# One copy of h's spectrum in HBM, a set order on GpSimd around the last group, and operand blocks in the place of u and v

## The chip, the cores and the metric

The kernel runs on one core of a Trainium2 chip. The metric is the device time of one execution in microseconds. Before the change it is 2052.42 us, the median of three runs (2049.76 to 2053.55). Every detail below comes from one further execution that was recorded by the hardware profiler.

The core's engines are named as in the profile: PE is TensorE (matrix products; PEld is its loading of weights), DVE is VectorE, ACT is ScalarE, POOL is GpSimd and SP is SyncE, which here only issues transfers. Each engine works through its own list of instructions in order. Transfers are issued by SP (one hardware queue, q1 in the profile) and by POOL (the software queue, q0).

## The reference

Two parts follow each other. The first is a long causal convolution of eight sequences (5696 tokens, 128 channels) with one filter per channel. The second turns each value by an angle that depends on the token, mixes all tokens with two 5696 x 5696 matrices, and ends with a small layer over channels.

```python
L = 2 * S
Xf = np.fft.rfft(x, n=L, axis=1)
Hf = np.fft.rfft(h, n=L, axis=0)
Yf = Xf * Hf[None, :, :]
y = np.fft.irfft(Yf, n=L, axis=1)[:, :S, :]

theta = y @ w_theta
zr, zi = y * np.cos(theta), y * np.sin(theta)
yr = np.einsum('ts,bsd->btd', w_tok_r, zr)
yi = np.einsum('ts,bsd->btd', w_tok_i, zi)
u = y + yr + yi
out = u + np.maximum(u @ w_ch, 0.0)
```

## The kernel before

**The convolution** (0 to about 395 us) is a Fourier transform of 11392 points, written as matrix products: 178 by 64 points, of which 90 frequencies of the long factor are kept. Work goes in eight groups: two batches (`bp`) times half of the channels (`dh`, 64 of 128), in the order of `groups` (L127). Each group goes through four stages. Stage a (L241 to 258) multiplies x by the first transform's matrix (L250). Stage b (L395 to 410) does the second factor (`f2`, L268), copies the result to `xs` (L402) and multiplies it by h's spectrum `hs`, once as it is and once with its halves swapped, into `u_t` and `v_t` (L404). Stage c (L412 to 431) transforms back (L422, L423), stage d (L433 to 460) finishes and writes the result `yt` (L448). While a group is in its stages c and d, the next group's stages a and b are woven between (`woven`, L278; L729 and L738).

`load_x(g)` (L130) fetches a group's x in 16 transfers on POOL, in narrow rows, into a tile of which there is one only. So the loads of a group wait until TensorE has read the last of the group before.

**h's spectrum** is computed once for all 128 channels. The half for the first 64 channels goes to `hs`. The half for the other 64 (`h_later`) goes to HBM, to `hf_hbm`, by `h_store` (L335): each chunk is written twice, as it is and with its two 64-row halves exchanged, since stage b needs both. When group 3 has used `hs` for the last time with the first half of the channels, each chunk is overwritten by one load from `hf_hbm` (L408).

**The phase steps** (L680) take 128 tokens and four batches each: a transpose by TensorE (L693), five groups of products that give the angle with its whole turns removed (L519 to L536), sine and cosine on ACT (L541 to L543), two products on DVE that give `zz` (L554, L555). A copy of the transposed y goes to HBM as `y2` (L698, L699). The 22 steps of the first four batches (`steps0`, `hh` = 0) stand among the last group's stages c and d and right behind; they read `ya0` and store zz to `z_hbm` (L572). The 22 steps of the other four batches (`steps1`, `hh` = 1) read `ya1`, whose last quarter comes straight from the last group's `yt` (`load_ya1`, L660: two transfers at L673 on SP). The rest of `yt` goes to `yt_hbm` on POOL, behind a one-element copy on POOL that is called the gate (L453 to L459) and that waits for ya1.

**Mixing** takes the rest. Weight tiles come from HBM into a ring of six slots (`load_w`, L625: four transfers on POOL for each slot; for the first six slots a one-element copy stands ahead that waits for a `zz`, L630), are transposed by DVE (L831) and multiplied with the operand blocks `b0` to `b10` (L1137, later L1216). A block holds the zr and zi of its tokens. `load_b_half` (L763) loads the half that the steps of `hh` = 0 have left in `z_hbm`; the steps of `hh` = 1 write their half straight into the blocks (L568). The products of the first blocks are interleaved with the steps of `hh` = 1. Block 0 lies in the ring's tile; blocks 1 to 6 come from a pool opened at L744 and get their places in the order in which they are asked for, at the earliest free address. In the profiled execution block 7's place fell into the space of `ya0`.

**What sets the order.** A scheduler orders each engine's instructions, except on the engines and in the stretches that `tc.manual_schedule` names, where the order of the program stays. Around the last group POOL is in the scheduler's hands, so a load can be put ahead of a copy that stands before it in the program. The transfers of each queue use eight semaphores in turn, so that an issue also waits for the transfer eight before it.

Of the kernel before, what the change touches and what calls it, by code (L numbers as in the profile page):

```python
# [23 lines left out]
def kernel(  # L24
# [66 lines left out]
    CN = 10  # L91
    CHN = [(c0, min(CN, N2 - c0)) for c0 in range(0, N2, CN)]
    UVW = 2 * HD * K1
    hf_hbm = nc.dram_tensor("hf_hbm", (P, UVW), F16, kind="Internal").ap()
    yt_hbm = nc.dram_tensor("yt_hbm", (D, B, S), BF16, kind="Internal").ap()

    psp = ExitStack()
# [221 lines left out]
    def halves(t, c, n, lo=0):  # L319
        return t[:, 2 * HD * CHK[c][0] - lo:2 * HD * (CHK[c + n - 1][0] + CHK[c + n - 1][1]) - lo].rearrange(  # L320
            "p (c r n) -> p c r n", c=n, r=2)
# [11 lines left out]
            nc.sync.dma_start(own[p0:p0 + 64, :, 1], own[64 - p0:P - p0, :, 0])  # L333

    def h_store(c, n):  # L335
        to = halves(hf_hbm, c, n)
        own = h_later[:, HD * CHK[c][0]:HD * (CHK[c + n - 1][0] + CHK[c + n - 1][1])].rearrange(
            "p (c n) -> p c n", c=n)
        nc.sync.dma_start(to[:, :, 0], own)
        for p0 in (0, 64):  # L340
            nc.sync.dma_start(to[p0:p0 + 64, :, 1], own[64 - p0:P - p0])

    r_u = fc.tile([P, P], F16)
    r_v = fc.tile([P, P], F16)
# [50 lines left out]
    def stage_b(a_st, warm, refill):  # L395

        def chunk(c):
            c0, ck = CHK[c]
            hv = h_part(c)
            ps = f2(a_st, c, warm)  # L400
            xs = fs.tile([P, 2, HD, CK], F16, tag="xs", name="xs")
            nc.scalar.activation(xs[:, :, :, :ck], ps, AF.Copy)  # L402
            for r in range(2):
                nc.vector.tensor_tensor(  # L404
                    uv[r][:, :, :, c0:c0 + ck], xs[:, :, :, :ck],
                    hv[:, r:r + 1].to_broadcast([P, 2, HD, ck]), op=mult)
            if refill:
                nc.sync.dma_start(h_flat(c),  # L408
                                  hf_hbm[:, 2 * HD * c0:2 * HD * (c0 + ck)])
        return [lambda c=c: chunk(c) for c in range(NCK)]  # L410

    def stage_c(st, last):  # L412
# [20 lines left out]
    def stage_d(st, bp, dh, then=None):  # L433
        def chunk(n0, cn):
            if n0 == 0:
                st["yt"] = fy.tile([P, NB, N2], BF16, tag="yt", name="yt")
            g_, yt = st["g"], st["yt"]
            ps = psum()
            nq = 5 if cn == CN else cn
            for j in range(cn):  # L440
                n = n0 + j
                o = ps[:, j // nq, (j % nq) * NB:(j % nq + 1) * NB]
                for ri in range(2):
                    e_ = e_t[:K1, n, ri, :] if n < EN else e_t[:K1, N2 - n, ri, ::-1]
                    nc.tensor.matmul(o, g_[:K1, ri * N2 + n, :], e_, start=(ri == 0), stop=(ri == 1))
            y_out = yt[:, :, n0:n0 + cn].rearrange("p m (a q) -> p m a q", q=nq)
            y_in = ps[:, :cn // nq, :nq * NB].rearrange("p a (q m) -> p m a q", q=nq)
            nc.scalar.activation(y_out, y_in, AF.Copy)  # L448
            if n0 + cn == N2:
                if then is not None:  # L450
                    then(yt)
                if then is not None:
                    gate = nc.gpsimd.tensor_copy(small(0, 1)[HD:HD + 1], sides["phases"][1][HD:HD + 1, 3, H - 1:H]).ins  # L453
                for e in range(2):
                    t0 = H if then else 0
                    with tc.issue_after(gate) if then else ExitStack():
                        (nc.gpsimd if then else nc.sync).dma_start(
                            yt_hbm[dh * HD:(dh + 1) * HD, 2 * bp + e, t0:],
                            yt[64 * e:64 * e + 64].rearrange("p m n -> p (m n)")[:, t0:])  # L459
        return [lambda n0=n0, cn=cn: chunk(n0, cn) for n0, cn in CHN]  # L460

    zz_n, rm_n = [0], [0]
# [22 lines left out]
    for n, f in enumerate(a0):  # L485
        f()
        if n == 9:
            e_table(*E_STEPS[0])
    e_index(*E_STEPS[4])
    load_x(1)  # L490
    in_order.close()
    in_order.enter_context(tc.manual_schedule(engines={mybir.EngineType.DVE, mybir.EngineType.Activation}))
    woven(b0, ([s_table, lambda: r_table(0, r_u), lambda: r_table(1, r_v)], 0.0, 0.6),
# [121 lines left out]
    def small(at, n):  # L615
        return ring["all"][:, WB + BT + at:WB + BT + at + n]
# [43 lines left out]
    def load_ya1(yt=None):  # L660

        st = sides["phases"]
        if yt is None:
            a_ = fa.tile([P, 2 * K1, HD], F16, tag="a", name="ya1")
            ya = st[1] = a_.rearrange("p k d -> p (k d)")[:, :4 * H].bitcast(BF16).rearrange(
                "p (b t) -> p b t", b=4)
            for p_ in range(2):
                nc.sync.dma_start(ya[:, :2, p_ * 2 * QR:(p_ + 1) * 2 * QR],
                                  yt_hbm[:, 4:6, p_ * 2 * QR:(p_ + 1) * 2 * QR])
            nc.sync.dma_start(ya[:HD, 2:], yt_hbm[:HD, 6:8, :H])  # L670
        else:
            for e in range(2):
                nc.sync.dma_start(st[1][HD:, 2 + e, :],  # L673
                                  yt[64 * e:64 * e + 64].rearrange("p m n -> p (m n)")[:, :H])

    M2, M6, M7, M5, M1, M3, M4 = range(7)
    ORDER = (M3, M4, M5, M2, M1, M7, M6)
    home_of = {}

    def phase_step(ti, hh):  # L680

        st = sides["phases"]
        yT = st[hh][:, :, ti * P:(ti + 1) * P]
# [12 lines left out]

        def copy():
            nc.vector.tensor_copy(y_ap, tpz)  # L698
            (nc.gpsimd if hh else nc.sync).dma_start(y2_hbm[ti].rearrange("p b d -> p (b d)")[:, 512 * hh:512 * hh + 512],  # L699
                          y_ap.rearrange("p b d -> p (b d)"))  # L700

        phases_b(ti, y_ap, 4 * hh, 4, yT, None, None, None, nc.vector, st["turns"], theta_ps=theta_ps,
# [2 lines left out]
    tile_order = []  # L705
    for a in range(6):
        tile_order += [ti for ti in (a, 5 + a, 11 + a, 16 + a) if ti < 22 and ti not in tile_order]
    steps0 = [lambda ti=ti: phase_step(ti, 0) for ti in tile_order]

    def with_load(step, load):  # L710
        def both():
# [3 lines left out]
                pump()  # L715
        return both

    for g, (bp, dh) in enumerate(groups):
        st = {}
        last = g + 1 == len(groups)  # L720
        a_, b_ = front(g + 1, () if g else (5, 11))
        if last:
            for _ in range(3):
# [20 lines left out]
    bpe = [ctx.enter_context(tc.tile_pool(name="bpool_e", bufs=1, side="right", reuse_waits="tile"))]  # L744
    bts_of = {0: [], 1: []}

    def tile_b(p, j, pool):
        t_ = ring["all"][:, WB:WB + BT] if j == 0 else pool.tile([P, BT], BF16, tag=f"b{j}", name=f"b{j}")
        bt = [t_[:, k * 1024:(k + 1) * 1024].rearrange("p (r n) -> p r n", r=2) for k in range(7)]
        bts_of[p].append(bt)  # L750
        return t_
# [527 lines left out]
```

## Time and profile before

| | us |
|---|---|
| median of three runs | 2052.42 |
| profiled execution | 2055.21 |
| its span, first to last instruction | 2053.4 |
| TensorE busy | 1948.2 (95%) |
| VectorE busy | 1574.1 (77%) |
| ScalarE busy | 653.6 (32%) |
| GpSimd busy | 968.2 (47%) |

The mean granted TensorE clock was 0.985 of full speed. A line of a timeline gives the start, the busy time, the engine (a q behind its name: the issue of a transfer), the line of the kernel, the operation, the tile written and the tiles read, the number of instructions taken together, and in brackets the idle time before, with what ended it. By stretches, with TensorE's busy time in each, the clock, and the mean busy share of the core's 16 DMA engines:

| stretch, us | PE busy, us | clock | DMA share |
|---|---|---|---|
| 55 to 60 | 2.20 of 5 | 0.53 | 1.91 |
| 60 to 65 | 0.02 of 5 | 0.50 | 1.73 |
| 65 to 71 | 1.57 of 6 | 0.50 | 0.78 |
| 335 to 350 | 13.56 of 15 | 1.00 | 0.86 |
| 350 to 365 | 12.46 of 15 | 1.00 | 1.19 |
| 395 to 410 | 9.90 of 15 | 0.77 | 0.95 |
| 410 to 425 | 10.31 of 15 | 0.77 | 1.02 |
| 455 to 470 | 12.56 of 15 | 0.94 | 0.94 |

A share above 1 means that transfers overlap in the records of an engine.

### The profile page before, as it was taken

Reading aid. Unit: us, or ns where it says so; the run is one execution under the profiler, and the core shown is the slowest. Engines: PE = TensorE matmul, PEld = TensorE weight load, DVE = VectorE, ACT = ScalarE, POOL = GpSimd, SP = SyncE. Lnnn points to the kernel's source line nnn. Section 1 sums busy time; section 2 is a strip of 40 time slices with the busy share of each in tenths; the row PEclk is TensorE's granted clock in tenths of the full one; section 3 lists DMA queues with packets and bytes.
Section 4 is the critical chain, followed back from the end, with each engine's and each line's share of the span. In section 5 each row is a group of like instructions: output and inputs, shape, how many; then the busy total and the mean of one; then the engine's idle time right before and its main releaser. Section 6 shows DMA issues by size and latency. Waiting matters only on the chain.

```text
span 2053.4 us, 41419 instructions
## 1 busy us (share of the span) xinstructions
PE 1948.2 (95%) x15841; PEld 1072.1 (52%) x15841; DVE 1574.1 (77%) x2890; ACT 653.6 (32%) x1004; POOL 968.2 (47%) x1738
## 2 busy tenths in 40 slices
PE   5699999789999999999999998999999999999998
PEld 5588888544444444444444443444444444444444
DVE  8677778767788888888867667867777686777767
ACT  6688888852333333333300000011111111111111
POOL 9422422274454545454566454453544535354450
PEclk9899999999999999999999999999999999999999
DMA  9968966999999998989999799697887969788793
GB/s 111 95 74 132 88 81 174 221 257 195 170 171 181 169 181 153 181 170 179 170 172 159 117 250 220 105 153 131 149 147 128 157 125 153 131 151 145 128 160 84
DMA packets 492486, 314.03 MB, mean 153 GB/s; under 512 B 182599, under 2 KB 456391, under 8 KB 491303
## 3 DMA queue, kind: packets, MB, share of 16 engines
q0 software_dynamic: 322208, 156.75, 60.5%
q1 hardware_dynamic: 164096, 143.10, 24.4%
q10 hardware_dynamic: 5984, 11.54, 1.6%
q8 instruction: 124, 2.03, 0.4%
q14 instruction: 74, 0.61, 0.1%
HBM read 354.89 MB, written 92.29 MB: 218 GB/s over the span
## 4 chain that ended last, share of the span: by engine, by line
PE 67%; DVE 3%; POOL 1%; issue 1%; DMA 1%; ACT 0%; DVEq 0%; POOLq 0%
PE m L1216 61%; PE m L1137 2%; POOL ring L632 1%; DVE c L1223 1%; DVE b L772 1%; PE utp L911 1%; PE v L918 1%; PE m L1220 1%; DVE wt L831 1%; PE theta_ps L519 0%; PE tpz L859 0%; PE m L1103 0%; DMA wl<-in_moe_w_tok_i_dram 0%; DMA y_hbm<-ring 0%; POOL wl L878 0%
## 5 line engine op out<-in xcount | busy, mean ns | idle before, releaser
L632 POOL DMA_DIRECT2D ring<-in_moe_w_tok_i_dram x720 | 388.1, 547 | 658.2 <-DVE wt L831 576.5
L632 POOL DMA_DIRECT2D ring<-in_moe_w_tok_r_dram x720 | 386.6, 548 | 147.6 <-DVE wt L831 81.6
L831 DVE STREAM_TRANSPOSE wt<-ring 128x384 f32<-128x384 f32 (+2 forms) x720 | 359.9, 525 | 111.9 <-PE m L1216 71.2
L1216 PE MATMUL m<-b,wt 128*128 128x512 bf16 x1640 | 390.5, 380 | 2.0 <-DVE wt L831 1.7
L1216 PEld LDWEIGHTS <-wt 128*128 128x128 bf16 x1804 | 176.5, 98 | 220.1 <-DVE wt L831 7.8
L1223 DVE TENSOR_TENSOR c<-c,m 128x512 f32<-128x512 f32 x412 | 266.0, 671 | 0.4 <-PE m L1216 0.4
L913 ACT ACTIVATE ring<-utp 128x512 bf16<-128x512 bf16 x85 | 50.7, 597 | 582.2 <-PE utp L911 582.2
L137 POOL DMA_DIRECT2D x<-in_x_dram x128 | 99.3, 801 | 140.6 <-PE ps L250 133.3
L422 PE MATMUL ps<-r_u,u_t 128*128 128x128 f16 x1024 | 125.1, 221 | 9.3 <-ACT ph L542 3.4
L423 PE MATMUL ps<-r_v,v_t 128*128 128x128 f16 x1024 | 124.2, 220 | 0.3
L1137 PE MATMUL m<-b,wt 128*128 128x512 bf16 x480 | 113.9, 388 | 10.3 <-DMA b<-z_hbm 5.7
L908 ACT ACTIVATE ub<-c 128x512 bf16<-128x512 f32 x88 | 55.1, 628 | 191.5 <-DMA ring<-in_moe_w_tok_r_dram 112.9
L423 PEld LDWEIGHTS <-v_t 128*128 128x128 f16 x1024 | 100.8, 99 | 7.2 <-issue 6.0
L422 PEld LDWEIGHTS <-u_t 128*128 128x128 f16 x1024 | 100.9, 99 | 5.2 <-DVE u_t L404 4.0
L402 ACT ACTIVATE xs<-ps 128x1024 f16<-128x1024 f32 x96 | 91.8, 988 | 7.2 <-DVE v_t L404 1.6
L1137 PEld LDWEIGHTS <-wt 128*128 128x128 bf16 x528 | 51.6, 100 | 70.2 <-issue 12.2
L404 DVE TENSOR_TENSOR u_t<-xs,hs 128x1024 f16<-128x1024 f16 x96 | 64.0, 666 | 29.7 <-ACT xs L402 26.9
L521 ACT ACTIVATE red<-theta_ps,magic 128x512 f32<-128x512 f32 (+1 forms) x46 | 31.6, 687 | 134.3 <-PE theta_ps L519 97.6
L861 ACT ACTIVATE ring<-tpz 128x512 bf16<-128x512 bf16 (+1 forms) x46 | 27.5, 597 | 130.5 <-PE tpz L859 111.3
L268 PEld LDWEIGHTS <-w_t 64*128 64x128 f16 x3240 | 57.5, 99 | 21.8 <-issue 15.9
L250 PE MATMUL ps<-f_t,x 89*128 89x180 f16 x512 | 53.7, 247 | 11.4 <-DMA x<-in_x_dram 9.4
L404 DVE TENSOR_TENSOR v_t<-xs,hs 128x1024 f16<-128x1024 f16 x96 | 63.4, 661 | 0.0
(2934 smaller groups left out, 3812.1 us busy)
## 6 DMA issues: line engine op xcount, KB each, us to landing
ring<-in_moe_w_tok_r_dram POOLq DMA_DIRECT2D x352, 96.0 KB, 4.6
ring<-in_moe_w_tok_i_dram POOLq DMA_DIRECT2D x352, 96.0 KB, 4.8
ring<-in_moe_w_tok_r_dram POOLq DMA_DIRECT2D x352, 80.0 KB, 4.3
ring<-in_moe_w_tok_i_dram POOLq DMA_DIRECT2D x352, 80.0 KB, 3.7
cp_hbm<-c SPq DMA_DIRECT2D x88, 256.0 KB, 2.4
c<-cp_hbm SPq DMA_DIRECT2D x88, 256.0 KB, 4.5
out_dram<-c SPq DMA_DIRECT2D x88, 256.0 KB, 4.0
yy<-y_hbm SPq DMA_DIRECT2D x84, 128.0 KB, 2.4
```

The costliest lines, as they stand in the source:

```text
L137: nc.gpsimd.dma_start(x16[p0:p1, e, n0:n0 + 16, :HD], bass.AP(tensor=src.tensor, offset=src.offset + (p0 * N2 + n0) * D + dh * HD, ap=[[N2 ...
L268: nc.tensor.matmul(ps[:, e, j * HD:(j + 1) * HD], w_t2[rows, slot(e, c0 + j), N2 * (1 - ri):N2 * (3 - ri)], a_st["a"][rows, ri * K1 + c0 + ...
L402: nc.scalar.activation(xs[:, :, :, :ck], ps, AF.Copy)
L404: nc.vector.tensor_tensor(uv[r][:, :, :, c0:c0 + ck], xs[:, :, :, :ck], hv[:, r:r + 1].to_broadcast([P, 2, HD, ck]), op=mult)
L422: nc.tensor.matmul(o, u_t[:, at:at + P], r_u, start=True, stop=False)
L423: nc.tensor.matmul(o, v_t[:, at:at + P], r_v, start=False, stop=True)
L632: nc.gpsimd.dma_start(wb[32 * i:32 * i + 32, :ng, :nj * 64], bass.AP(tensor=a.tensor, offset=a.offset + row0 * S + p * H + i * QR + j0 * 6 ...
L831: nc.vector.transpose(wt.rearrange("p j t r -> p (j t r)").bitcast(F32).rearrange("p (j g t) -> p g j t", j=TJ, g=4)[:, :ng, :nj], wb[:, : ...
L908: nc.scalar.activation(ub[:m].rearrange("p b d -> p (b d)"), c[:m], AF.Copy)
L1137: nc.tensor.matmul(ms[n // 2 * 2 + h], a[n][:, j, :, r], bts_of[p][jj][n % 2 * 2 + h][:, r, :], start=(n % 2 == 0 and jj == 0 and r == 0), ...
L1216: nc.tensor.matmul(ms[q], a[q][:, j, :, r], bts[jj][q][:, r, :], start=(jj == 0 and r == 0), stop=(jj == NJ - 1 and r == 1 and q not in left))
L1223: nc.vector.tensor_tensor(c, z, ms[q], op=op)
```

## The change

Five things change, all in front of the mixing part:

1. `h_store` writes the second half's spectrum once, in four plain stores; `hf_hbm` is half as large. The reload in group 3 makes the swapped half: three loads for a chunk instead of one.
2. `load_x(1)` stands ahead of the index set `e_index(*E_STEPS[4])` on POOL.
3. From the last group to the end of the steps of `hh` = 0, POOL keeps the order of the program (`late_order`). The gate of L453 is gone.
4. The two `ya` loads from `yt`, and the y2 stores of the steps 12 to 16 of `hh` = 0, are issued by POOL and no longer by SP.
5. The tiles of blocks 1 to 6 are asked for in the order 5, 6, 1, 2, 3, 4, before the loads, which stay in the order 0 to 6. Blocks 1 to 4 thereby get the addresses that `u_t` and `v_t` had.

The order of instructions on DVE and ACT stays. On PE the products on block 1 begin inside the fourth step of `hh` = 1 and no longer behind the sixth; some thirty groups later the two orders agree again. POOL issues the loads of block 1 directly behind the y2 store of the first step of `hh` = 1.

```diff
-    hf_hbm = nc.dram_tensor("hf_hbm", (P, UVW), F16, kind="Internal").ap()
+    hf_hbm = nc.dram_tensor("hf_hbm", (P, HD * K1), F16, kind="Internal").ap()
...
     def h_store(c, n):
-        to = halves(hf_hbm, c, n)
-        own = h_later[:, HD * CHK[c][0]:HD * (CHK[c + n - 1][0] + CHK[c + n - 1][1])].rearrange(
-            "p (c n) -> p c n", c=n)
-        nc.sync.dma_start(to[:, :, 0], own)
-        for p0 in (0, 64):
-            nc.sync.dma_start(to[p0:p0 + 64, :, 1], own[64 - p0:P - p0])
+        part = slice(HD * CHK[c][0], HD * (CHK[c + n - 1][0] + CHK[c + n - 1][1]))
+        nc.sync.dma_start(hf_hbm[:, part], h_later[:, part])
...
             if refill:
-                nc.sync.dma_start(h_flat(c),
-                                  hf_hbm[:, 2 * HD * c0:2 * HD * (c0 + ck)])
+                src = hf_hbm[:, HD * c0:HD * (c0 + ck)]
+                nc.sync.dma_start(h_flat(c)[:, :HD * ck], src)
+                for p0 in (0, 64):
+                    nc.sync.dma_start(h_flat(c)[p0:p0 + 64, HD * ck:], src[64 - p0:P - p0])
...
                     then(yt)
-                if then is not None:
-                    gate = nc.gpsimd.tensor_copy(small(0, 1)[HD:HD + 1], sides["phases"][1][HD:HD + 1, 3, H - 1:H]).ins
                 for e in range(2):
                     t0 = H if then else 0
-                    with tc.issue_after(gate) if then else ExitStack():
-                        (nc.gpsimd if then else nc.sync).dma_start(
+                    (nc.gpsimd if then else nc.sync).dma_start(
...
+    load_x(1)
     e_index(*E_STEPS[4])
-    load_x(1)
...
             for e in range(2):
-                nc.sync.dma_start(st[1][HD:, 2 + e, :],
+                nc.gpsimd.dma_start(st[1][HD:, 2 + e, :],
...
-    def phase_step(ti, hh):
+    def phase_step(ti, hh, store=nc.sync):
...
-            (nc.gpsimd if hh else nc.sync).dma_start(y2_hbm[ti].rearrange("p b d -> p (b d)")[:, 512 * hh:512 * hh + 512],
+            store.dma_start(y2_hbm[ti].rearrange("p b d -> p (b d)")[:, 512 * hh:512 * hh + 512],
...
-    steps0 = [lambda ti=ti: phase_step(ti, 0) for ti in tile_order]
+    steps0 = [lambda ti=ti, n=n: phase_step(ti, 0, nc.gpsimd if 12 <= n < 17 else nc.sync)
+              for n, ti in enumerate(tile_order)]
...
+    late_order = ExitStack()
     for g, (bp, dh) in enumerate(groups):
         st = {}
         last = g + 1 == len(groups)
+        if last:
+            late_order.enter_context(tc.manual_schedule(engines={mybir.EngineType.Pool}))
...
+    place_of = {}
+
+    def new_b(j, pool):
+        return ring["all"][:, WB:WB + BT] if j == 0 else pool.tile([P, BT], BF16, tag=f"b{j}", name=f"b{j}")
+
     def tile_b(p, j, pool):
-        t_ = ring["all"][:, WB:WB + BT] if j == 0 else pool.tile([P, BT], BF16, tag=f"b{j}", name=f"b{j}")
+        t_ = place_of.pop(j) if j in place_of else new_b(j, pool)
...
+    for j in (5, 6, 1, 2, 3, 4):
+        place_of[j] = new_b(j, home_pool(j))
     for j in range(7):
         load_b_half(j)
     for step in steps0:
         step()
+    late_order.close()
...
-    steps1 = [lambda ti=ti: phase_step(ti, 1) for ti in
+    steps1 = [lambda ti=ti: phase_step(ti, 1, nc.gpsimd) for ti in
```

More of the change, by code (lines that the diff above doesn't have):

```diff
@@ L451, in chunk @@
                     then(yt)
-                if then is not None:
-                    gate = nc.gpsimd.tensor_copy(small(0, 1)[HD:HD + 1], sides["phases"][1][HD:HD + 1, 3, H - 1:H]).ins
                 for e in range(2):
                     t0 = H if then else 0
-                    with tc.issue_after(gate) if then else ExitStack():
-                        (nc.gpsimd if then else nc.sync).dma_start(
-                            yt_hbm[dh * HD:(dh + 1) * HD, 2 * bp + e, t0:],
-                            yt[64 * e:64 * e + 64].rearrange("p m n -> p (m n)")[:, t0:])
+                    (nc.gpsimd if then else nc.sync).dma_start(
+                        yt_hbm[dh * HD:(dh + 1) * HD, 2 * bp + e, t0:],
+                        yt[64 * e:64 * e + 64].rearrange("p m n -> p (m n)")[:, t0:])
         return [lambda n0=n0, cn=cn: chunk(n0, cn) for n0, cn in CHN]
@@ L672, in load_ya1 @@
             for e in range(2):
-                nc.sync.dma_start(st[1][HD:, 2 + e, :],
-                                  yt[64 * e:64 * e + 64].rearrange("p m n -> p (m n)")[:, :H])
+                nc.gpsimd.dma_start(st[1][HD:, 2 + e, :],
+                                    yt[64 * e:64 * e + 64].rearrange("p m n -> p (m n)")[:, :H])
     M2, M6, M7, M5, M1, M3, M4 = range(7)
```

## The prediction

> **What bounds the kernel now.** I read the page's totals and its chain first:
>
> ```profile
> span 2053.4 us, 41419 instructions
> PE 1948.2 (95%) x15841; PEld 1072.1 (52%) x15841; DVE 1574.1 (77%) x2890; ACT 653.6 (32%) x1004; POOL 968.2 (47%) x1738
> ...
> PE 67%; DVE 3%; POOL 1%; issue 1%; DMA 1%; ACT 0%; DVEq 0%; POOLq 0%
> PE m L1216 61%; PE m L1137 2%; POOL ring L632 1%; DVE c L1223 1%; DVE b L772 1%; PE utp L911 1%; PE v L918 1%; PE m L1220 1%; DVE wt L831 1%; PE theta_ps L519 0%; PE tpz L859 0%; PE m L1103 0%; DMA wl<-in_moe_w_tok_i_dram 0%; DMA y_hbm<-ring 0%; POOL wl L878 0%
> ```
>
> TensorE is busy for 95%, and the mixing products of L1216 are 61% of the chain. The change does not touch that part; what it can win is TensorE's idle time before it, and a microsecond won there shifts the rest. So I took timelines of two places where TensorE waits, first the wait for the second group's x:
>
> ```profile
> 43.25 0.47 PE L250 MATMUL ps<-f_t,x 89*128 89x180 f16 x4 [0.20 <-ACT a__745 L257]
> ...
> 43.30 0.57 POOL L155 IOTA e_all<- 90x445 f32 x1
> 43.98 0.64 POOL L375 TENSOR_SCALAR e_all<-e_all,lane 90x445 f32<-90x445 f32 x1
> 44.70 1.33 POOL L159 TENSOR_SCALAR e_all<-e_all 90x445 f32<-90x445 f32 x1
> 45.98 6.21 POOL L137 DMA_DIRECT2D x<-in_x_dram  x8
> ...
> 62.80 0.61 POOL L137 DMA_DIRECT2D x<-in_x_dram  x1 [0.23 <-DMA x<-in_x_dram]
> ...
> 65.12 0.38 DVE L404 TENSOR_TENSOR v_t<-xs,hs 128x256 f16<-128x256 f16 x1
> ...
> 69.43 2.00 PE L250 MATMUL ps<-f_t,x 89*128 89x180 f16 x12 [9.41 <-DMA x<-in_x_dram]
> 71.22 0.31 PE L422 MATMUL ps<-r_u,u_t 128*128 128x128 f16 x1
> ```
>
> The index set (three GpSimd operations) stands ahead of the 16 x loads, TensorE waits 9.41 us for the last of these, and stage c (L422), whose operands were complete at 65.5, starts at 71.22. The queues from 44 to 70 us, where h's stores (q1) run beside x (q0):
>
> ```profile
> q0 software_dynamic: 12544, 1.46, 90.4%
> q1 hardware_dynamic: 3584, 3.11, 45.7%
> ```
>
> Then the transition to mixing:
>
> ```profile
> 394.91 0.70 SPq L673 DMA_DIRECT2D ya<-yt  x1
> ...
> 399.23 0.29 PE L693 MATMUL tpz<-ident_bf,ya 128*128 128x128 bf16 x1 [2.92 <-DMA ya<-yt]
> ...
> 401.32 0.39 DVE L698 COPY ring<-tpz 128x512 bf16<-128x512 bf16 x1
> ...
> 407.78 4.32 POOL L767 DMA_DIRECT2D b<-z_hbm  x8 [2.60 <-PE theta_ps L536]
> ...
> 414.69 1.86 PE L1137 MATMUL m<-b,wt 128*128 128x512 bf16 x4 [5.46 <-DMA b<-z_hbm]
> ...
> 422.33 1.03 PE L1137 MATMUL m<-b,wt 128*128 128x512 bf16 x4
> ```
>
> TensorE waits 2.92 us for ya and 5.46 us for the first operand block; the loads of the blocks start only at 407.78, when ya0's last reader (L536) has freed the place of block 7, which stands first.
>
> **The change part by part.** *Set order and h's bytes.* The index set's 2.7 us (43.30 to 46.0) move behind the x loads. These can't start before TensorE's last read of the single x buffer (43.25 + 0.47 = 43.7), so they start 2.2 us earlier. h's 12 stores of 2.95 MB become 4 of 1.47 MB. x(2), loaded with nothing beside it, needs 16 us from first issue (86.97) to the last landing; x(1) needs 23.4. I put the 7.4 us between down to h, and halve them with its bytes: 3.7. x(1) would land at 43.7 + 16 + 3.7 = 63.4, 6.0 us earlier. Next in line is the last v_t at 65.5; with 0.1 us to start, stage c moves from 71.2 to 65.6, its four batches of x products first filling TensorE's wait: **-5.6 us**. Bounds: -2.2 (order alone, h's bytes unfelt) and -5.7. The moved set ends some 2.7 us after x's last issue, at 63.9 even if x's 17.4 us of issuing stay; its reader on VectorE starts at 65.4: 0, and up to +1 if that cover fails. SP's queue only gets shorter here.
>
> *Refill.* 12 loads become 36, in group 3, at 172.9 to about 194. At 0.55 to 0.6 us an issue they are 21 us of SP, behind which two stores of yt wait (before, the last ends at 194.3). Landing takes these up to 7.9 us, and ACT overwrites yt at 212.6; the refilled hs is read at 210.8. Cover of some 10 us: **0**; +3 if the swapped halves go at half speed.
>
> *Ring order of the last group.* Ten of the 24 first ring loads were issued at 338.9 to 344.7, ahead of the copies that gate the rest. Now all follow their gates, from 350.2. The transfers beside them (yt's stores, ya1, y2) then start against an emptier queue, and 350 to 360 gets fuller: from 350 to 365 the DMA share is already 1.19, from 335 to 350 it is 0.86. VectorE waits for y2 stores in these rows, 3.2 us at 361.43 and 1.0 at 364.02. **-1**; bounds -4 (both waits gone) and +2 (as many ring loads as now, later, in the fuller stretch).
>
> *ya and the operand blocks.* yt is complete at 391.5. GpSimd, idle there, can issue the two ya loads at once, ending at 392.7 instead of 395.6 behind z's and y2's stores on SP; with the 3.8 us that ya takes to land, 396.5 instead of 399.2. VectorE gains nothing by that: it is busy without a gap from 392.6 to 401.3, so the first y2 copy of the second half stays at 401.3. Its store, GpSimd's next instruction, issues at 402.3, and b1 behind it at 402.9 instead of 408.4, since block 1 lies where u_t was and waits for no ya0. From issue to landing b1 took 6.3 us (408.4 to 414.7): 409.2. But TensorE's order changes too: the first product on b1 now stands inside the fourth step, three steps earlier. Behind it come the 7.6 us from 414.7 to 422.3 plus three steps of five phase groups at 0.22 us, 3.3 us: 420.1, a gain of 2.2 at a place from which the two orders agree. In those 7.6 us groups took 0.42 us instead of 0.22 (granted clock 0.5); if the shorter wait leaves half of that slowness out, 2.5 us less. I take **-3.5**. Bounds: 0 (b1 lands at 411.4, so 420.1 becomes 422.3) and -8 (landing after 4.9 us, the median of the nearest 128 KB stores on that queue, and no slow stretch).
>
> [...]
>
> *Stores that change queue.* Five y2 stores and two ya loads leave SP, 7 x 0.6 = 4.2 us there, and add 0.55 to 0.6 each to GpSimd, idle 370 to 399 (29.1 us for ya), when most are issued. GpSimd later runs from 427 to 465 almost without pause, about 15 us behind VectorE at 419; loads that begin 5.5 us earlier shrink this. From 455 on TensorE waits 2.54 us for a weight block and 0.94 and 1.15 for the last operand rows, VectorE 1.56 and 1.45 for stores: 4.6 us of TensorE's. **-2**; bounds 0 and -4.
>
> Sum: -5.6 - 1 - 3.5 - 2 = -12.1 against the profiled execution, 2055.2 (span 2053.4), which lies 0.14% above the median of 2052.4. Taken from the median: **2041** (rounded up from 2040.3).
>
> **The rivals.** *Only the front gains.* b1 is asked for earlier and lands at 411 or later, the y2 waits stay: 2052.4 - 5.6 = 2047. For it: a share near 1.0 and b loads with a median of 7.9 us. Against: block 1 waits for no ya0 any more.
>
> *x's own issue is the limit.* If x's 16 loads keep 23.4 us (its own queue is 90.4% of the engines there), only 2.2 us are won in front: 2052.4 - 2.2 - 6.5 = 2044. Against it: the same loads took 16 us alone.
>
> *Stalls go entirely.* TensorE idles 10.7 us between 394 and 415 (1.87, 2.92, 0.42, 5.46). With the tail's 4.6 and 5.6 in front, at most 21; one that gives all but the ACT-bound 1.87 ends at 2033.
>
> *Slower: the software queue is full when b1 comes.* Ahead of b1 it holds ya and yt, 0.7 MB each, b0 0.5 and y2 0.1, 2.1 MB from 391.5 on, and block 1 itself has 0.5. From 340 to 425 this queue moved 7.46 MB, 11.4 us a MB. At that pace the 2.1 MB are through at 415.4, b1 at 421 and b2, which TensorE needs 1 us after b1, at 427. b2's place in the old order is 417.5; being 9.5 us late there, with the three steps of 3.3 us still behind, costs 12.8, against 8.6 won elsewhere: 2057. It decides when b1 lands at 424 or b2 at 426 (411.4 + 8.6 + 4.1, and two more): then more than all the gains is eaten. Against: that pace was set by what was asked; h's 3.11 MB in 45.7% of 26 us make 3.8 us a MB, 8 us for the 2.1 MB, gone by 402.
>
> [...] The granted clock is 0.50 from 60 to 71 us after TensorE stopped, and 0.52 from 71 to 76. [...]
>
> **How the numbers follow.** Chances: the forecast, 2035 to 2046, 0.54; only the front 0.14; x's issue 0.11; stalls gone 0.09; slower 0.12. What tells from no change here is 0.2%, 4.1 us, so faster means below 2048.3. Half of "only the front" ends within it or beyond, and some of x's: faster 0.76, same 0.11, slower 0.13. The range takes in the stalls-gone end in part and the front alone, 2031 to 2051.
>
> **What would show it.** In front: hardware-queue bytes of 1.6 MB in 44 to 70, x(1) landed by about 63.5, L422 first at 65.6. At group 3: 36 issues and no new wait at 210.8. In the last group: no ring load before 350, VectorE's waits at 361 shorter. Transition: ya issued by GpSimd at 391 to 393, b1 at 402.9 and landed by 409, TensorE's wait there under 5 us; mixing starts 10 us earlier by 475. The forecast is wrong if x(1)'s landing follows its own queue, if TensorE meets b1 before 405 and idles till 411, or if the first weight blocks come late because all 24 are gated.

## The result, and the profile after

The changed kernel takes 2043.61 us (median of 13 runs, 2040.61 to 2050.63), the kernel before 2054.64 us in the runs beside it (13 runs, 2049.76 to 2058.85). The ratio is 0.9954, with a 95% interval of 0.9941 to 0.9967, so 9.5 us less (6.8 to 12.1). The forecast was 2041 in a range of 2031 to 2051, and faster. The profiled execution took 2043.46 us, 11.75 us less than that of before.

The page of the changed kernel, its span and the engines' busy times:

```profile
span 2041.7 us, 41287 instructions
...
PE 1938.2 (95%) x15664; PEld 1074.5 (53%) x15841; DVE 1573.3 (77%) x2890; ACT 654.2 (32%) x1004; POOL 973.8 (48%) x1744
```

TensorE's share is what it was. Its busy time can't be set against that of before: this trace has 15664 records of products, that of before 15841 (the weight loads are complete in both). Where the time went is read from the timelines. The first place, in that of the changed kernel:

```profile
44.57 6.20 POOL L137 DMA_DIRECT2D x<-in_x_dram  x8 [1.41 <-PE ps L250]
...
61.69 1.00 DVE L400 TENSOR_TENSOR u_t<-xs,hs 128x1024 f16<-128x1024 f16 x1
...
62.24 1.66 POOL L159 TENSOR_SCALAR e_all<-e_all 90x445 f32<-90x445 f32 x1
...
63.40 2.20 PE L250 MATMUL ps<-f_t,x 89*128 89x180 f16 x12 [2.85 <-DMA x<-in_x_dram]
66.47 0.29 PE L420 MATMUL ps<-r_u,u_t 128*128 128x128 f16 x1 [0.87 <-DVE u_t L400]
```

TensorE waits 2.85 us for x instead of 9.41, and then 0.87 us for `u_t`; stage c (L420 here) starts 4.75 us earlier. The queues in 44 to 70 us (packets, MB, share of the 16 engines' time):

```profile
q0 software_dynamic: 12544, 1.46, 91.5%
q1 hardware_dynamic: 855, 1.60, 20.5%
```

x's queue is unchanged; the queue of h's stores has 855 packets in place of 3584, and they take 20.5% of the engines' time in place of 45.7%. The transition:

```profile
386.12 1.07 POOL L668 DMA_DIRECT2D ya<-yt  x2 [1.78 <-ACT yt L446]
...
388.23 1.12 POOL L771 DMA_DIRECT2D ring<-z_hbm  x2
396.31 0.55 POOL L694 DMA_DIRECT2D y_hbm<-ring  x1 [6.96 <-DMA z_hbm<-zz]
396.89 3.73 POOL L771 DMA_DIRECT2D b<-z_hbm  x7
...
392.88 0.23 PE L688 MATMUL tpz<-ident_bf,ya 128*128 128x128 bf16 x1 [2.26 <-DMA ya<-yt]
...
398.91 1.01 PE L1144 MATMUL m<-ring,wt 128*128 128x512 bf16 x2 [2.75 <-DMA ring<-z_hbm]
...
402.98 1.01 PE L1144 MATMUL m<-b,wt 128*128 128x512 bf16 x2 [0.72 <-DMA b<-z_hbm]
```

Block 1 is there at 403 instead of 414.7. A wait that was not there before has come: 2.75 us for block 0 (in the ring's tile), whose loads stood 10 us behind ya and yt.

TensorE runs the same instructions in all these kernels, in the same order but for some groups between 405 and 451 us. So the start of an instruction can be subtracted between two traces, and this tells where a gain comes from better than two total times. Thirteen profiles beside the first of before, one of them a second one of the same kernel, allow it to be done against a spread. The table gives how far TensorE is ahead of the first profile of before (minus is earlier), at weight loads that there start at the times named. At 424.7 us all kernels have done the same set of weight loads.

| kernel | stage c, 71.1 | 331.4 | 372.0 | 392.0 | 424.7 | 506.3 |
|---|---|---|---|---|---|---|
| changed | -4.6 | -2.1 | -5.8 | -5.7 | -9.0 | -10.6 |
| before_again | -0.6 | -1.6 | -2.1 | -1.6 | -3.0 | -2.2 |
| front_part | -5.1 | -3.0 | -3.5 | -4.5 | -5.3 | -5.6 |
| x_order | 0.0 | 0.9 | 1.0 | 1.2 | -1.3 | -0.8 |
| h_once | -5.4 | -0.8 | -0.3 | 0.0 | -2.8 | -3.0 |
| late_part | 0.1 | 3.1 | -0.6 | -0.6 | -5.1 | -6.5 |
| no_x_order | -5.6 | -0.4 | -4.1 | -5.2 | -9.2 | -11.2 |
| no_place | -3.7 | -1.1 | -5.1 | -6.1 | -9.0 | -10.3 |
| ring_free | -4.6 | -2.3 | -1.5 | -2.5 | -6.7 | -7.4 |
| hold_order | -4.2 | 0.7 | -3.0 | -2.6 | -6.5 | -7.6 |
| both | -5.4 | -3.6 | -7.9 | -7.3 | -12.0 | -14.6 |
| block7_first | -4.9 | -0.8 | -5.1 | -5.9 | -4.2 | -5.2 |
| y2_back | -2.2 | -0.7 | -4.8 | -4.8 | -8.1 | -9.8 |

The runs are told below. In us, each ratio is taken times the median of before in the same comparison.

### The profile page after: what moved, and what is told of

Same layout as the page of the kernel before. It is cut to its first block, busy times and chain, and to the rows that moved or that the text cites. A ratio compares the mean times of both kernels' runs of the same rounds, so it can differ in the third digit from the quotient of the medians.

```text
span 2041.7 us, 41287 instructions
## 1 busy us (share of the span) xinstructions
PE 1938.2 (95%) x15664; PEld 1074.5 (53%) x15841; DVE 1573.3 (77%) x2890; ACT 654.2 (32%) x1004; POOL 973.8 (48%) x1744
## 4 chain that ended last, share of the span: by engine, by line
PE 63%; DVE 4%; DMA 3%; issue 2%; POOL 2%; ACT 0%; DVEq 0%; SPq 0%
PE m L1223 59%; POOL ring L627 2%; DVE c L1230 1%; DMA ring<-in_moe_w_tok_i_dram 1%; PE v L925 1%; PE utp L918 1%; PE m L1227 1%; DVE wt L838 1%; DVE b L776 1%; DMA ring<-in_moe_w_tok_r_dram 1%; PE theta_ps L514 0%; PE tpz L866 0%; DMA wl<-in_moe_w_tok_i_dram 0%; PE m L1110 0%; PE m L1144 0%
## 5 line engine op out<-in xcount | busy, mean ns | idle before, releaser
L1223 PE MATMUL m<-b,wt 128*128 128x512 bf16 x1599 | 385.0, 379 | 4.2 <-DVE wt L838 1.7
L420 PE MATMUL ps<-r_u,u_t 128*128 128x128 f16 x1024 | 125.6, 221 | 5.3 <-DVE u_t L400 2.4
L1144 PE MATMUL m<-b,wt 128*128 128x512 bf16 x465 | 109.8, 381 | 7.2 <-DMA b<-zz 2.7
L420 PEld LDWEIGHTS <-u_t 128*128 128x128 f16 x1024 | 101.2, 99 | 3.3 <-DVE u_t L400 3.3
L776 DVE TENSOR_TENSOR b<-b 128x1024 bf16<-128x1024 bf16 x100 | 61.4, 682 | 0.0
```

The costliest lines, as they stand in the source:

```text
L420: nc.tensor.matmul(o, u_t[:, at:at + P], r_u, start=True, stop=False)
L776: return [lambda f=f, x=x: f(*x) for f, x in ((nc.vector.tensor_sub, (bt[M3], b12, b22)), (nc.vector.tensor_sub, (bt[M4], b21, b11)), (nc. ...
L1144: nc.tensor.matmul(ms[n // 2 * 2 + h], a[n][:, j, :, r], bts_of[p][jj][n % 2 * 2 + h][:, r, :], start=(n % 2 == 0 and jj == 0 and r == 0), ...
L1223: nc.tensor.matmul(ms[q], a[q][:, j, :, r], bts[jj][q][:, r, :], start=(jj == 0 and r == 0), stop=(jj == NJ - 1 and r == 1 and q not in left))
```

## The experiments

### The front: bytes of h, or order of the loads

Two parts in front, together and each by itself, and the rest alone. The edit of `front_part` is parts 1 and 2 of the change on the kernel before, that of `late_part` parts 3 to 5. `x_order` is part 2 alone:

```diff
+    load_x(1)
     e_index(*E_STEPS[4])
-    load_x(1)
```

and `h_once` part 1 alone:

```diff
...
-        nc.sync.dma_start(to[:, :, 0], own)
-        for p0 in (0, 64):
-            nc.sync.dma_start(to[p0:p0 + 64, :, 1], own[64 - p0:P - p0])
...
+        nc.sync.dma_start(hf_hbm[:, part], h_later[:, part])
...
```

> Parts 1 and 2 of the change alone on the kernel before (one copy of h with the swapping reload, and x's loads ahead of the index set). Theory A (the forecast): the start of stage c comes 5 us earlier and all of it reaches the end, so about 5 us less in all. Theory B (from the trace of the changed kernel, where TensorE was 4.2 us ahead at 89 us but only 2.1 at 335): part of the gain is given back in groups 1 to 7, in waits that stand in both kernels, and 2 us less arrive. Both expect TensorE's wait for x near 2.9 us instead of 9.4 and x(1)'s last landing near 63.

> Parts 3 to 5 alone on the kernel before (GpSimd in the program's order around the last group, the stores and ya on GpSimd, the places of the blocks). Theory A: ring order -1, ya and blocks -3.5, tail -2, together -6.5 us. Theory B (from the changed kernel's trace): the ring order is worth more, -3.7 between 335 and 366 us, the rest as in A, together 9 us less. In both the front is as before, TensorE's wait for x 9.4 us.

> Only x's loads ahead of the index set, h stored twice as before. Theory A: x is issued 1.4 to 2.2 us earlier and lands as much earlier, TensorE's wait 7.5 us, total -2. Rival: with h's bytes unchanged the queues are as full as before, x keeps its 23.4 us from first issue to last landing, and the whole gain is the 1.4 us of its start. In both the index set, now beside VectorE's products, may slow some of these.

> Only the one copy of h with its swapping reload, order as before. Theory A: h's half of the bytes cost x 3.7 us, so x lands that much earlier, TensorE's wait is 5.7 us, total about -3.5. Rival: x's own queue (90% of the engines) is the limit and the wait stays 9 us. The refill shows 36 loads on SP from about 172 to 198 and costs nothing in either; if it costs, TensorE's start of the next group's stage b near 210 us comes later than the other marks.

| run | ratio to before | 95% interval | us |
|---|---|---|---|
| front_part | 0.9983 | 0.9971 to 0.9996 | -3.5 |
| late_part | 0.9964 | 0.9951 to 0.9976 | -7.4 |
| x_order | 0.9986 | 0.9974 to 0.9997 | -2.9 |
| h_once | 0.9971 | 0.9960 to 0.9982 | -6.0 |

The two halves of the change give -10.9 us, the whole -9.5: they add up within their intervals. The two parts of the front don't: alone they give -8.9 together, `front_part` only -3.5 (-0.8 to -6.0), and why is open. Nor do the totals decide between the two theories of `front_part` (5 or 3 us) and of `late_part` (6.5 or 9 us). So the parts are told from the traces. The timeline of `x_order`, at the wait for x:

```profile
69.40 2.00 PE L250 MATMUL ps<-f_t,x 89*128 89x180 f16 x12 [8.80 <-DMA x<-in_x_dram]
```

and of `h_once`:

```profile
63.32 2.00 PE L250 MATMUL ps<-f_t,x 89*128 89x180 f16 x12 [2.93 <-DMA x<-in_x_dram]
65.65 0.29 PE L420 MATMUL ps<-r_u,u_t 128*128 128x128 f16 x1 [0.33 <-DVE u_t L400]
```

With its loads issued 1.4 us earlier (44.6 us), x's last transfer still lands when it did, at 69.1. With one copy of h, x is used at 63.3, 6.1 us earlier, though issued at the old time. So the rival that x's queue alone is the limit falls, and the split of the forecast falls with it: h's stores are all of it, at this place. Their bytes (3.11 to 1.57 MB on that queue in `h_once`), their number (12 to 4) and their packets (3584 to 811) fell together, and no run tells which of these counts. The size agrees with the queues: 45.7% less 20.5% of 26 us are 6.6 us of packet time on each of the 16 engines, and x, last in line, came 6.1 us earlier. That is one case, and the two shares overlapped before (136% in sum). The total of `x_order` (-0.6 to -5.3 us) leaves room for a gain that its profile doesn't show; which of the two is nearer isn't settled by it, but the next run bears on it.

### Part 2 undone

`no_x_order` is the changed kernel with the two lines in their old order.

> The changed kernel with part 2 undone: the index set ahead of x's loads again. Theory A (the forecast's split, 2.2 us for this part) expects it 2 us slower than the changed kernel. Theory C, formed from the runs of the parts (x's loads ahead alone: TensorE's wait for x 8.8 us; one copy of h alone: 2.9 us), expects no loss: the bytes of h were all of it, and VectorE's products at 61 to 64 us, 1.0 us each beside the index set in the changed kernel, take 0.69 again, so that stage c starts near 65.6 instead of 66.5. Total 0 to -1 against the changed kernel.

The ratio to before is 0.9945 (0.9933 to 0.9958), 11.3 us less than before; the changed kernel's was 0.9954 (0.9941 to 0.9967). So by the totals nothing is lost without part 2. Stage c starts 5.6 us earlier than in the first profile of before, in the changed kernel 4.6. Over all profiles with one copy of h, leaving out `y2_back`, in which TensorE stood 2.05 us before 56.35 us in a gap that the trace puts down to issue, it is -5.3 on average in four with the old order (4.9 to 5.6) and -4.4 in five with the new (3.7 to 5.1). Part 2 costs about 0.9 us at stage c.

The price can be seen in the rows of the changed kernel above. GpSimd's index set runs at 59.7 to 63.9 us, in the middle of VectorE's products: two of these take 1.00 and 1.04 us instead of 0.69, and two of the three index operations 1.70 and 1.66 instead of 0.64 and 1.33. The same pair of slow products is in `x_order` (1.05 and 1.04), and none is in `h_once` or `no_x_order`. The last `u_t` ends at 66.4, and stage c, which waits for it, starts at 66.47.

The operations that run side by side lose time, and on both engines: GpSimd 1.06 and 0.33 us in two operations, VectorE 0.3 us each in two products, less than either index operation takes alone (0.64 and 1.33 us). What slows them no run shows.

### What the early start lost on its way

By 331 us the ten profiles with one copy of h had lost 3.2 us of their start at stage c on average (1.5 to 5.2), the four others 0.7 (gained 1.0 to lost 3.0). A second profile of the kernel before tells whether its first was a lucky one:

> The kernel before once more, for a second profile. In seven runs of other kernels TensorE lost 2 to 6 us of its lead between 78 and 335 us, also in the two whose front is as before (late_part and x_order fell 3.3 and 2.3 us behind the first profile of the kernel before). If the first profile of the kernel before had few of the waits that the trace calls issue (8.9 us of TensorE's in this stretch, against 9.6 to 13.6 in the others), the second one shows 10 to 13 us and lies 2 to 3 us behind the first at 335, and the lead was not given back by the change. If it shows 9 us again, the earlier front did cost something there.

TensorE's gaps that the trace puts down to issue add up to 10.2 us in 78 to 335 us of this profile, and to 8.9 in the first. In the four profiles with two copies of h they are 8.9 to 11.1 us (mean 9.9), in the ten with one copy 10.9 to 14.3 (mean 12.6). So the first profile was not far from the second, which lies 1.6 us ahead of it at 331 us and not 2 to 3 behind, and the expectation that the loss is only the luck of one profile fails: with an early front TensorE stands about 2.7 us longer in these gaps. Most come at the same places of TensorE's program (near 95 to 101 us, 134 to 141, 170 to 182 and 208 to 222), next to transfers of 16 KB on the queue that the page calls instruction; what TensorE waits for there no run shows.

The gaps are not all of it. The granted clock of TensorE stood at half for 3.4 to 13.7 us of this stretch in the four profiles with two copies of h (mean 8.5), and for 6.8 to 20.5 us in the ten with one (mean 11.9). Over the 14 profiles the loss goes with this time (correlation 0.88) more closely than with the gaps (0.69). `late_part`, whose front is as before, lost 3.0 us with gaps of 9.6 us, but 13.7 us at half clock; `both` lost 1.8 us with gaps of 12.7 us and only 6.8 us at half clock. Whether an earlier front brings on either, or these ten profiles had less luck, is open: the two groups overlap. A run that shifts the loads of x against TensorE's program, and nothing else, would be needed.

### The order of the ring loads

`ring_free` lets the scheduler order GpSimd until the last group's stage c is done:

```diff
-        if last:
-            late_order.enter_context(tc.manual_schedule(engines={mybir.EngineType.Pool}))
         a_, b_ = front(g + 1, () if g else (5, 11))
...
+        if last:
+            late_order.enter_context(tc.manual_schedule(engines={mybir.EngineType.Pool}))
         now = [steps0.pop(0) for _ in range(5)] if last else []
```

> The changed kernel, but GpSimd's program order begins only behind the last group's stage c, so ten ring loads go out at 337 to 343 us again, ahead of their gates, and the rest as changed. Theory A (ring order worth 1 us): total 1 us slower. Theory B (TensorE won 3.7 us between 352 and 366 us in the changed kernel): total 3 to 4 us slower, and TensorE's lead over the kernel before stays near what it is at 335 us until 380.

The ratio is 0.9969 (0.9957 to 0.9981), 6.4 us less than before, beside 11.3, 11.5 and 11.7 in the three other variants of the changed kernel that were measured with it on the same chip. The table shows it at its place: from 331 to 372 us the eight profiles with the new order gain 3.7 to 4.3 us on before, `ring_free` loses 0.8, and the four further ones with the old order lie between a gain of 0.5 and a loss of 0.6. Theory B holds.

The mechanism is that of the forecast, VectorE's waits for y2 stores. In the timeline of VectorE, first the kernel before, then the changed one, then `ring_free`:

```profile
361.43 0.42 DVE L698 COPY ring<-ps 128x512 bf16<-128x512 bf16 x1 [3.17 <-DMA y_hbm<-ring]
```

```profile
363.48 0.42 DVE L693 COPY ring<-ps 128x512 bf16<-128x512 bf16 x1 [0.74 <-DMA y_hbm<-ring]
```

```profile
359.99 0.42 DVE L693 COPY ring<-ps 128x512 bf16<-128x512 bf16 x1 [4.00 <-DMA y_hbm<-ring]
```

Before and in `ring_free` a second such wait follows, of 1.04 and 1.08 us; in the changed kernel none does. So 4.2 us of waits became 0.7, and TensorE gained 3.7 us there. By stretches of 15 us (length, then the busy times of PE, PEld, DVE, ACT and POOL, TensorE's clock, the DMA share and GB/s), the changed kernel ahead of `ring_free`:

```profile
348.00:363.00 15.00, 14.44 (x222) 12.94 (x223) 13.70 (x21) 14.16 (x26) 9.65 (x22) 1.00 1.14 271
```

```profile
348.00:363.00 15.00, 11.52 (x177) 10.52 (x179) 9.60 (x15) 10.37 (x18) 6.56 (x15) 0.99 1.19 278
```

TensorE is busy 2.9 us longer in the same stretch, while the transfers are nearly as dense. In 333 to 348 us a y2 store takes 8.1 us to land in the changed kernel; in the 335 to 350 us of before it took 10.9.

### The place of the blocks, or what stands ahead of them

`no_place` is the changed kernel without these lines, so that blocks 1 to 6 lie where they did:

```diff
-    for j in (5, 6, 1, 2, 3, 4):
-        place_of[j] = new_b(j, home_pool(j))
```

> The changed kernel with part 5 undone: blocks 1 to 6 placed in the order in which they are loaded. Theory A (the forecast's cause: block 1 came late because of its place) expects b1 several us later and the total 3 to 5 us slower. Rival D: before, b1 was late because the load of block 7 stood ahead of it on GpSimd and waited for ya0; in this kernel block 7 is behind, and block 1 in its old place waits only for transfers of yt and ya that were issued at 386 to 388 us and have landed when its load is issued at 397. Then TensorE meets b1 at the same 403 us and the total stays.

The ratio is 0.9944 (0.9931 to 0.9957), no slower than the changed kernel. TensorE meets block 1 at the same time:

```profile
403.29 1.01 PE L1142 MATMUL m<-b,wt 128*128 128x512 bf16 x2 [1.48 <-DMA b<-z_hbm]
```

So the place was not the cause. GpSimd stands 1.64 us ahead of block 1's loads here and TensorE waits 0.76 us longer than in the changed kernel; these rows show no more that the place would bring. The other side of the test is `block7_first`, in which blocks 1 to 4 lie in the new places and part 2 is undone, but the scheduler puts block 7's first load ahead of them again. It came with a move of block 0's load ahead of the last group's stage d:

```diff
+        if last:
+            load_b_half(0)
         now = [steps0.pop(0) for _ in range(5)] if last else []
...
-    for j in range(7):
+    for j in range(1, 7):
         load_b_half(j)
```

> The index set and block 0 as in the run both, but the loads of block 7, which wait for ya0's last reader and for the last z stores, stand ahead of the first y2 store and of block 1, as they do in the kernel before; blocks 1 to 4 lie where u and v were. Rival D (block 7 in front, not block 1's place, made block 1 late) expects GpSimd to stand before block 7 until about 402 to 404, block 1 to be issued 6 us later than in the changed kernel and to land near 410, and the total to lose 3 to 5 us against no_x_order. Theory A (the place counts) expects no loss.

```profile
399.72 1.12 POOL L742 DMA_DIRECT2D b<-z_hbm  x2 [11.66 <-DMA z_hbm<-zz]
...
407.08 1.01 PE L1147 MATMUL m<-b,wt 128*128 128x512 bf16 x2 [9.10 <-DMA b<-z_hbm]
```

GpSimd stands 11.66 us before block 7's loads, and TensorE then waits 9.10 us for block 1. From 392 to 425 us TensorE falls back by 1.7 us, where the changed kernel wins 3.3. The total is 0.9961 (0.9949 to 0.9974), 8.0 us less than before, 3.3 us more than `no_x_order`; the intervals of the two overlap, so that it is the trace that decides. Rival D holds: what made block 1 late was a load that nobody needed yet, which stood ahead on the same queue with a later release.

### The y2 store ahead of block 1, and block 0

`hold_order` closes `late_order` only in the mixing part, so that the loads of blocks 1 to 6 come ahead of the first y2 store of the second half:

```diff
-    late_order.close()
     sides["phases"]["ya0"].close()
...
             ordered.close()
+            late_order.close()
```

> The changed kernel, with GpSimd kept in program order past the first steps of the second half, so that the loads of blocks 1 to 6 stand ahead of the first y2 store of these steps. If what sets b1 in the changed kernel is that store (issued at 396.3, when VectorE's copy is done), b1 is issued near 390 and lands before 399, TensorE's wait for b1 and part of the half clock go, and the total is 2 to 4 us faster than the changed kernel. If the full software queue sets it (ya, yt and b0, 2 MB issued from 386 on), b1 lands at 402 as now and nothing is won; GpSimd, held by the loads of blocks 5 and 6 that wait for the last z stores until about 400, may then make the y2 stores late, 1 to 2 us slower.

The ratio is 0.9943 (0.9923 to 0.9963), 2.2 us below the changed kernel's, but the intervals overlap. GpSimd now issues block 1 directly behind block 0, 3 us after ya's issue, and TensorE no longer waits for it at all. But block 1 takes 11.4 us from issue to landing, where it took 6.1, and lands at 403.8; counted from ya's issue that is 14.6 us instead of 16.9. And TensorE waits for block 0 all the same:

```profile
392.44 1.65 POOL L771 DMA_DIRECT2D b<-z_hbm  x3
...
402.40 0.59 PE L1144 MATMUL m<-ring,wt 128*128 128x512 bf16 x2 [3.18 <-DMA ring<-z_hbm]
```

From 392 to 425 us it gains 3.9 us, the changed kernel 3.3; but the six profiles in which the store stands ahead and block 7 does not gain 2.8 to 4.5. So no gain is shown from taking the store out of the way, and of the two expectations the one by which the filled software queue sets block 1's landing came nearer. `both` has block 0 out of that queue as well: block 0 early (the diff of `block7_first`), `late_order` held, and part 2 undone.

> The changed kernel with the index set ahead of x's loads again (as in no_x_order), block 0's loads ahead of the y2 stores, ya and yt on GpSimd (about 371 us instead of 388), and the loads of blocks 1 to 6 ahead of the first y2 store of the second half. In the changed kernel and in hold_order TensorE waits 2.8 to 3.2 us for block 0, whose loads stand 10 us in a queue behind ya and yt. If this wait is what kept hold_order from winning, it is gone here and the total is 2 to 4 us below no_x_order. If not (ACT and VectorE, which pace the first steps of the second half, end the waits next), the wait moves to them and the total stays within 1 us.

```profile
368.30 1.12 POOL L742 DMA_DIRECT2D ring<-z_hbm  x2 [0.63 <-DMA z_hbm<-zz]
...
394.99 1.06 PE L1147 MATMUL m<-ring,wt 128*128 128x512 bf16 x2
...
399.68 0.69 DVE L549 TENSOR_TENSOR zz<-ph,ring 128x512 bf16<-128x512 f32 x1 [3.59 <-DMA z_hbm<-zz]
...
403.21 0.59 PE L688 MATMUL tpz<-ident_bf,ya 128*128 128x128 bf16 x4 [2.39 <-DVE ring L693]
```

The waits for blocks 0 and 1 are gone, and 392 to 425 us gives 4.7 us, a little more than the 2.8 to 4.5. The wait that takes their place is VectorE's, 3.59 us for a `zz` buffer whose store to `z_hbm` is still on its way, and TensorE waits 2.39 us for VectorE behind it. The ratio is 0.9939 (0.9921 to 0.9958): 12.5 us less than before, the best of these kernels, with a median of 2041.49 us. Against `no_x_order` it is 1.2 us, less than the intervals can tell; its profile is 4.0 us ahead of the changed kernel's at 506 us, 1.5 of them won by 331, and the times do not show that it beats it.

### The five y2 stores

`y2_back` has them on SP again.

```diff
-    steps0 = [lambda ti=ti, n=n: phase_step(ti, 0, nc.gpsimd if 12 <= n < 17 else nc.sync)
+    steps0 = [lambda ti=ti, n=n: phase_step(ti, 0, nc.sync)
```

> The changed kernel with the five y2 stores of the steps 12 to 16 on SP again; ya stays on GpSimd. The forecast gave the stores and ya together 2 us, most of it late, from 425 on. If SP's queue counts, z's stores and with them block 0 and 1 come 1 to 3 us later and the total is 1 to 2 us slower; if not, it is unchanged within 1 us.

0.9960 (0.9947 to 0.9973), 8.2 us less than before: 1.3 us less gain than the changed kernel, which the intervals don't tell apart. In the table it has the same steps as the changed kernel, -3.4 from 392 to 425 us and -1.6 from there to 506. So by the trace the queue of these five stores is worth less than 1 us up to there.

## Why the prediction was right, and where it was not

Direction, range and size were right: -12.1 in the forecast, -11.75 between the two profiled executions, -9.5 (6.8 to 12.1) by the ratio. That the sum fits so well is luck in part, since two terms behind it were wrong in opposite directions by 2.4 to 2.9 us each. In the last column the mean over the profiles with the part is set against the mean over those without, so that the first profile of before counts as one among several (from 392 us on, `hold_order`, `both` and `block7_first` are left out; in 392 to 425 us the other profiles with the old order were 0.8 to 2.8 us faster than it):

| term | forecast | changed, its profile | by means |
|---|---|---|---|
| start of stage c | -5.6 | -4.6 | -4.3 with part 2, -5.2 without |
| given back, 71 to 331 us | 0 | 2.5 | 2.4 |
| ring order, 331 to 372 | -1 | -3.7 | -3.9 |
| ya and blocks, 392 to 425 | -3.5 | -3.3 | -2.2 |
| stores, tail, 425 to 506 | -2 | -1.6 | -1.6 |

The changed kernel's profile won a further 1.1 us behind 506 us.

*Set order and h's bytes.* The end was nearly right (stage c at 66.5 instead of 65.6), and x was in use at 63.4, to the tenth as forecast, by luck: the working was not right. The step that failed is "I put the 7.4 us between down to h, and halve them with its bytes: 3.7", and beside it 2.2 us for the order. h's price was 6.1 us and the order's nothing: in `x_order` the loads that were issued 1.4 us earlier landed when they did. The lone x(2) was a poor yardstick, since GpSimd spent 12.3 of its 16 us issuing it without a pause. The drop of the other queue's packet time in that window (6.6 us) comes close to the price, and the fence of the two queues had one half of it. The rival "x's own issue is the limit" is refuted by `h_once`. The limit at 65.5 was right, `h_once` starts at 65.65.

That the index set costs "0, and up to +1 if that cover fails" had its bound right and its reason not: the reader did not wait for it, VectorE's products beside it were slowed. And "a microsecond won there shifts the rest" was too much: 2.5 of some 4.5 us were lost again by 331.

*Refill.* Right: 36 issues from 170.4 to 197.3 us, landing in 3.4 us at the median, yt's two stores issued by 198.6 and landed 8.9 us later, ACT's next write of yt at 210.2, and no wait for any of them.

*Ring order.* The mechanism was right, the term mis-sized: -1 in the forecast, -3.9 measured, at the bound of -4 that stood for both waits gone. The value was taken nearer to the other end because 350 to 365 us would get fuller; it did not (a share of 1.14, before 1.19), and the y2 stores issued ahead of it landed in 8.1 us instead of 10.9, which took most of VectorE's waits away.

*ya and the operand blocks.* The size was nearly right by the one profile (-3.3), two thirds of it by the means (-2.2), and both causes were partly wrong. yt was complete 5.7 us earlier than before, and the transposes that wait for ya start 6.35 us earlier: the move of ya to GpSimd is worth 0.7 us and not 2.7 (0.9 by the means: 6.9 us from yt's end to these transposes in the nine profiles with the move, 7.8 in the five without). Its landing took 5.0 us at the median and 6.2 at most, not 3.8, with yt's 720 KB directly behind; z's stores took 7.5 us there, before 3.4. That block 1 came early "since block 1 lies where u_t was" is refuted by `no_place`; block 7's load ahead was the cause, which the view of the transition had named and the working then dropped. Block 1 came at 403.0, 6.1 us after its issue, where 6.3 were taken. The wait of 2.75 us for block 0, and VectorE's 2.20 us for z stores behind it, were not foreseen. The DMA share over all queues was 0.86 to 0.99 in 388 to 403 us, with the moved transfers in it.

The clock fell to 0.58 in 393 to 398 us, to 0.50 in 398 to 403 and 0.55 in 403 to 408, so the slow stretch did not go; it was full in 408 to 413. In all it lasted 13.7 us, as long as the two of before together, so that the 2.5 us that the forecast put on it in part were not won here. TensorE's waits around its start were 1.88, 2.26 and 2.75 us, each shorter than the 5.46 us of before, and the clock fell all the same; in the 3.4 us ahead of the fall (390.4 to 393.8) TensorE was busy for 1.1 us.

*Stores and tail.* Right in size; `y2_back` shows that the five stores are not what does it. Which of the other parts does was not tried.

"Only the front gains" (5.6 us less) lies outside the interval, and `late_part` gains 7.4 us without the front. The slower rival did not come about: block 0 was there at 398.9 and block 1 at 403.0, 21 us before the point at which it would have decided.

## What to carry to other kernels

To price the removal of a transfer, look at the packet time that its queue takes from the engines in the window in which another one is waited for (here 6.6 us, for a gain of 6.1; one case), and don't count on a load landing earlier because it is issued earlier beside a busy queue (here 1.4 us earlier won nothing). When a load comes late, look first at what stands ahead of it on its issuing engine and what that waits for, and only then at its buffer. And compare the start of the same instruction in several traces, of the old kernel too: here two terms were wrong by 2.4 to 2.9 us and the total hid it. Set the time at half clock beside the waits when the same program loses differently from run to run.

## What the runs showed of the hardware that was not expected

TensorE stands 9 to 14 us in all between 78 and 335 us in gaps that no semaphore explains, most of them at the same places of its program in 14 profiles and up to 3.7 us each, next to 16 KB transfers of the instruction queue. They were longer (12.6 us on average against 9.9) in the kernels whose front is earlier.

A GpSimd operation on one 90x445 tile slowed from 0.64 us (before) to 1.70 (changed) beside VectorE's half-precision products, and the products from 0.69 to 1.04.

In the 14 profiles the granted clock fell to half 78 times between 60 and 520 us, and stayed there for 3.4, 6.8, 10.2 or 13.7 us. In the 3.4 us ahead of such a fall, as long as the shortest of these stretches, TensorE was busy for 0 to 63% (median 38%), and in only 7 of the cases was there a gap of 3.4 us or more; in the 1661 stretches of that length, counted on from the clock's last change, in which it stayed full, TensorE was busy for 41% or more.
